# A fused causal attention and PReLU MLP on one core: loads on three queues, a second round of its own, PReLU partly on ScalarE, stores by halves

## The chip, the cores and the metric

One core of one Trainium2 chip. The metric is the device time in microseconds (us) of one execution; each kernel is timed in several runs, and one further execution is profiled. Engines are called PE (TensorE), DVE (VectorE), ACT (ScalarE), POOL (GpSimd) and SP (SyncE, which here only issues DMAs).

## The reference

Causal attention over 4 batches of 12 heads, 448 positions and head size 64, then an MLP on 1792 tokens: 768 inputs, 2048 hidden, PReLU with one slope for each hidden unit, 768 outputs. All in float32.

```python
scores = (1/sqrt(64)) * q @ k.T ; masked above the diagonal with -1e9
attn = exp(scores - max) / (sum + 1e-9)
x = (attn @ v), heads side by side: (1792, 768)
h = x @ w_in
g = maximum(h, 0) + alpha * minimum(h, 0)
out = g @ w_out
```

## The kernel before

**Attention.** The 24 pairs of heads (two heads share the 128 partitions) are worked off in rounds. `ORDER` (L36) is one round's list of steps, each with a lag: `S0+1` in round n is the first scores of pair n - 1, `AV+4` the product with V of pair n - 4. Each engine works in the order in which its instructions are written, so this list is the queue of each engine. `LK` and `LQ` load K and Q on SP (`load`, L345: two DMAs for K, four for Q with its last 64 rows); pair 0's K is issued by ACT. `MXij` is DVE's masked row maximum (L429), `EXij` ACT's exponential with the row sum (L444), `RC` the reciprocal of the sums (L453), `NOij` the normalization on POOL (L398; for the first and the last pair partly on DVE, L460), `PTi` PE's transposes (L472), `Cij` their copies out of PSUM, `AV` the product (L491), `XF`, `XN`, `XH`, `XL` sums, high part and low part of the result. Round 2 uses the same list as the others. `WARM` matmuls on zeros (L338) run before the first scores.

**V.** A batch's V is loaded by seven DMAs (`load_v`, L370), all issued by SP. The first seven follow `LQ` of pair 2; the others are issued in `LV`, by the table `LOADV` (the number after pair p).

**Weights.** Every matmul of the MLP is three matmuls of high and low parts in fp32r. w_in and w_out come as eight-byte numbers, of which pieces of 128x384 are turned to float32 by `start_piece` (L231): an Abs on ACT, a clamp on POOL, four bit operations on DVE (`D`; L249, L253, L256, L257), an add on POOL (`+` or `add`, L260). `cast` (ACT) and `sub` (POOL) make high and low parts. During attention the tables `EARLY`, `FRONT` and `REAR` say in which round this is done (steps `ED`, `E2`, `EA`). `T` makes high and low part of a sum of x (`t_hi`, `t_lo`).

**MLP.** Hidden units come in 8 groups of 256, tokens in two blocks (384 and 512 columns): 16 quads. The first two quads are plain products (`h_plain`), the others seven products per four by sums (`h_step`). `h_act` (L709) makes PReLU of a PSUM bank with two DVE operations (L721, L722), `g_hi` the high part on ACT (L731), `g_lo` the low part on POOL (L735). `o_half` (L758) multiplies with w_out and adds on DVE (L777; for the first group a copy on ACT, L775). `FIRST` is the list of what goes between the products of the first two quads, one row for each product: `act`, `gh`, `gl` ahead of it, the rest behind; `th` and `tl` are the two halves of `T`, on ACT and DVE (L569). With the last group `o_half` stores: a whole row block of 768 columns behind its second half, only the very last block by halves (L778 to L785).

Of the kernel before, what the change touches and what calls it, by code (L numbers as in the profile page):

```python
# [10 lines left out]
F32 = mybir.dt.float32  # L11
# [12 lines left out]
WARM = 9  # L24
EARLY = {
# [92 lines left out]
def kernel(  # L118
# [23 lines left out]
    GC = 2  # L142
# [26 lines left out]
    alpha_sb = const.tile([P, DFF // P], F32, name="alpha_sb")  # L169
    OPS = ["B11", "T1", "T2", "B21", "T3", "B22", "T4"]  # L170
# [410 lines left out]
    plan, front, behind_it = {}, {}, {}  # L581
# [6 lines left out]
    for nm in "qk":  # L588
        steps["L" + nm.upper()] = lambda p, nm=nm: p and load(p, nm)
# [13 lines left out]
    steps["ED"] = lambda p: [fn() for fn in plan.pop(p + 4, ())]  # L603
    steps["LT"] = lambda p: p + 4 < 27 and flush(late)
# [3 lines left out]
    order = []  # L608
    for w in ORDER.split():
        name, lag = w.split("+")  # L610
        if name in choice:
            eng = {"a": nc.scalar, "d": nc.vector, "p": nc.gpsimd}[lag[-1]]
            order.append((int(lag[:-1]), name, lambda p, fn=choice[name], eng=eng: fn(p, eng)))
# [95 lines left out]
    def h_act(q, nm):  # L709
# [11 lines left out]
        ts(out=m, in0=src, scalar1=0.0, scalar2=al, op0=ALU.min, op1=ALU.mult)  # L721
# [36 lines left out]
    def o_half(q, n, t, hf):  # L758
# [105 lines left out]
    def plan_early():  # L864
# [4 lines left out]
        for table, to in ((EARLY, plan), (FRONT, front), (REAR, behind_it)):  # L869
            for n, todo in table.items():  # L870
                for w in todo.split():
# [3 lines left out]
                    if kind == "D":  # L875
                        fns.append(lambda i=int(arg[0]), n=int(arg[1]): ops(name_of(i), 0, n))
# [26 lines left out]
    with tc.manual_schedule():  # L903
# [173 lines left out]
```

## Time and profile before

| | us |
|---|---|
| median of 3 runs | 630.48 (628.66 to 632.01) |
| profiled execution | 627.45 |
| its span | 625.7 |
| PE, DVE, POOL, ACT busy | 608.4, 501.7, 395.7, 277.2 |

The page's first part gives the busy time of each engine; a share near 100% of PE says that PE always had a matmul in work, not that each ran at its fastest. The chain that ended last is 82% PE.

### The profile page before, as it was taken

To read this page: it belongs to the slowest core of one execution; us is meant where nothing else is said; L and a number is where in the kernel's file an instruction comes from. 1 tells how busy PE (TensorE), PEld (TensorE's weight loads), DVE (VectorE), ACT (ScalarE), POOL (GpSimd) and SP (SyncE) were. 2 spreads that over 40 slices of the span, in tenths; PEclk is the share of its full clock that TensorE was granted. 3 is DMA by queue.
4 is the path that set the end of the run, shared out by engine and by line. 5 is a ranking of instruction groups with operands and counts; after the bars stand their busy time and mean duration, and the time that the engine had idled before them with its cause. 6 is when DMAs were issued, how large, how long until landed. Compare 5 with 4: busy or idle time off the path is not lost.

```text
span 625.7 us, 10851 instructions
## 1 busy us (share of the span) xinstructions
PE 608.4 (97%) x3528; PEld 529.6 (85%) x3528; DVE 501.7 (80%) x1117; ACT 277.2 (44%) x766; POOL 395.7 (63%) x530
## 2 busy tenths in 40 slices
PE   7899999999999899999999999999999999999996
PEld 3566676666878799899999999989999999999896
DVE  5699999999688579798689879868977987895363
ACT  5789897898344655231333323232332323232110
POOL 4455676868776758865775687567667766763120
PEclk9899999999999999999999999999999999999999
DMA  5874477642868468656765775786667567554535
GB/s 130 194 184 135 117 223 208 204 134 70 281 188 287 136 207 288 212 181 204 246 190 176 230 215 155 222 250 177 191 221 221 179 218 224 166 175 140 178 137 201
DMA packets 87736, 120.39 MB, mean 192 GB/s; under 512 B 12032, under 2 KB 64256, under 8 KB 87680
## 3 DMA queue, kind: packets, MB, share of 16 engines
q1 hardware_dynamic: 87520, 119.48, 62.6%
q8 instruction: 28, 0.46, 0.3%
q10 hardware_dynamic: 160, 0.23, 0.1%
q14 instruction: 28, 0.23, 0.1%
HBM read 105.00 MB, written 14.68 MB: 191 GB/s over the span
## 4 chain that ended last, share of the span: by engine, by line
PE 82%; DVE 6%; DMA 4%; SPq 3%; POOL 2%; ACT 1%; issue 1%; POOLq 0%; ACTq 0%; DVEq 0%
PE o L769 35%; PE heldY L676 11%; PE heldX L676 8%; PE heldZ L676 5%; PE pt L472 5%; PE a L491 4%; PE s L417 3%; PE h_V L676 3%; PE heldW L676 2%; DMA v<-in_v_dram 2%; PE s L409 2%; SPq L352 2%; ACT p L444 1%; SPq L355 1%; DVE s L429 1%
## 5 line engine op out<-in xcount | busy, mean ns | idle before, releaser
L777 DVE TENSOR_TENSOR acc<-o,acc 128x384 f32<-128x384 f32 x196 | 107.5, 552 | 71.2 <-PE o L769 70.9
L398 POOL TENSOR_SCALAR p<-p,rs 128x128 f32<-128x128 f32 (+3 forms) x164 | 80.4, 512 | 57.2 <-DVE rs L453 34.4
L444 ACT ACTIVATE p<-s,nm 128x256 f32<-128x256 f32 (+3 forms) x168 | 82.0, 497 | 20.1 <-DVE nm L429 19.8
L769 PE MATMUL o<-wo,g_X 128*128 128x384 f32 x336 | 76.8, 335 | 2.9 <-ACT g_X L731 1.8
L769 PE MATMUL o<-wo,g_Z 128*128 128x384 f32 x336 | 76.6, 335 | 1.1 <-DVE t_W L722 0.6
L429 DVE CUSTOM_DVE_ANT_0 s<-s,mask 128x256 f32<-128x256 f32 (+3 forms) x168 | 70.9, 480 | 8.0 <-PE s L417 5.7
L769 PE MATMUL o<-wo,g_W 128*128 128x384 f32 x336 | 76.6, 334 | 0.3 <-POOL g_W L735 0.3
L769 PE MATMUL o<-wo,g_Y 128*128 128x384 f32 x336 | 76.4, 335 | 0.0
L769 PEld LDWEIGHTS o<-wo,g_X 128*128 128x128 f32 x336 | 60.3, 188 | 6.7 <-ACT g_X L731 2.1
L769 PEld LDWEIGHTS o<-wo,g_Z 128*128 128x128 f32 x336 | 60.2, 188 | 4.9 <-DVE t_W L722 0.9
L769 PEld LDWEIGHTS o<-wo,g_W 128*128 128x128 f32 x336 | 59.9, 188 | 0.6 <-POOL g_W L735 0.6
L769 PEld LDWEIGHTS o<-wo,g_Y 128*128 128x128 f32 x336 | 60.0, 188 | 0.0
L491 PEld LDWEIGHTS a<-ptf,v 128*64 128x64 f32 x384 | 27.7, 136 | 35.1 <-issue 10.5
L472 PEld LDWEIGHTS pt<-ident,p 128*128 128x128 f32 x384 | 44.6, 144 | 13.7 <-issue 10.9
L491 PE MATMUL a<-ptf,v 128*64 128x64 f32 (+3 forms) x384 | 49.5, 387 | 3.6 <-DMA v<-in_v_dram 2.3
L472 PE MATMUL pt<-ident,p 128*128 128x128 f32 x384 | 48.7, 279 | 2.4 <-DVE p L460 1.3
L260 POOL TENSOR_TENSOR y_i<-y_i,x_i 128x384 f32<-128x384 f32 x32 | 33.5, 1048 | 27.1 <-DVE x_i L257 27.1
L260 POOL TENSOR_TENSOR y_o<-y_o,x_o 128x384 f32<-128x384 f32 x32 | 32.4, 1012 | 15.9 <-DVE x_o L257 15.9
L394 ACT ACTIVATE ptf<-pt 128x512 f32<-128x512 f32 (+1 forms) x72 | 38.3, 574 | 8.6 <-PE pt L472 8.6
L735 POOL TENSOR_TENSOR g_Z<-t_Z,g_Z 128x384 fp32r<-128x384 f32 (+1 forms) x16 | 20.0, 1247 | 31.1 <-ACT g_Z L731 31.1
L417 PE MATMUL s<-kr,qr 64*128 64x128 f32 (+2 forms) x288 | 38.4, 394 | 0.0
L243 ACT ACTIVATE x_i<-raw_i 128x384 f32<-128x384 f32 x32 | 17.8, 555 | 46.3 <-DMA raw_i<-in_moe_w_in_dram 46.3
(177 smaller groups left out, 1339.4 us busy)
## 6 DMA issues: line engine op xcount, KB each, us to landing
lo_T<-low_T SPq DMA_DIRECT2D x28, 512.0 KB, 4.6
lo_B<-low_B SPq DMA_DIRECT2D x25, 512.0 KB, 4.7
raw_i<-in_moe_w_in_dram SPq DMA_DIRECT2D x32, 384.0 KB, 3.8
raw_o<-in_moe_w_out_dram SPq DMA_DIRECT2D x32, 384.0 KB, 3.3
lo_T<-low_T SPq DMA_DIRECT2D x28, 384.0 KB, 3.9
lo_B<-low_B SPq DMA_DIRECT2D x25, 384.0 KB, 3.9
lo_N<-low_N SPq DMA_DIRECT2D x16, 512.0 KB, 4.8
lo_N<-low_N SPq DMA_DIRECT2D x16, 384.0 KB, 4.5
```

What stands on the lines that cost most here:

```text
L260: nc.gpsimd.tensor_tensor(out=y, in0=y, in1=xf, op=ALU.add)
L394: eng.activation(out, x, AF.Copy, scale=side)
L398: eng.tensor_scalar(out=out, in0=x, scalar1=side, scalar2=1.0, op0=ALU.mult, op1=ALU.mult)
L417: nc.tensor.matmul(ps[:, o : o + lim], T["q", p][half(j), i * QP : (i + 1) * QP], T["k", p][half(j), :lim], start=(o == 0), stop=(n > 0 or ...
L429: nc.vector.tensor_tensor_reduce(out=t, in0=t, in1=masks[1] if i == NQ else masks[0][:, (NQ - 1 - i) * QP :], scale=-SCALE, scalar=MOST_F3 ...
L444: nc.scalar.activation(T["p", p, i][:, j, : t.shape[1]], t, AF.Exp, scale=-1.0, bias=T.pop(("nm", p, i, j)), accum_out=T["sm", p][:, z : z ...
L472: nc.tensor.transpose(ps[:, j - js[0], c], t[:, j, c * QP : (c + 1) * QP], T["ident"])
L491: nc.tensor.matmul(out[half(j), c * QP :], vs[b % 2][:, hp, c, j], x[:, c * QP : S], start=(c == 0), stop=(c == NQ),)
L676: nc.tensor.matmul(ps, w[:, u, k * P : (k + 1) * P], x, start=(first and i == 0), stop=(i == len(mms) - 1), skip_group_check=True,)
L735: nc.gpsimd.tensor_tensor(out=l, in0=hts.pop((q, nm)), in1=h, op=ALU.subtract)
L769: nc.tensor.matmul(ps[:, :NH], x, w, start=(i == 0), stop=(i == 3 * GC - 1))
L777: nc.vector.tensor_tensor(out=a[:, cols], in0=ps[:, :NH], in1=a[:, cols], op=ALU.add)
```

## The change

`WARM` goes from 9 to 8. The K of pair 1 is issued by ACT too. The first four V loads are issued by POOL after `LQ` of pair 1, the other three by SP after `LQ` of pair 2. Round 2 has a list of its own. A new step `EG` takes the first bit operation of a round where the round's work begins with one; `ED` moves behind `RC`. Some entries of `EARLY` and `FIRST` move, and V's last batch is loaded in three rounds. For six of the eight PReLUs of the first group, ACT makes alpha * min(h, 0) as Relu(-h) times -alpha (`less`). `g_lo` of the second quad goes to DVE but for Y. Every half row block is stored as soon as it is done.

```diff
-WARM = 9
+WARM = 8
 EARLY = {
-    13: "+:0 D:1:2 A:2 cast:A21", 14: "C:2 D:1:1 LD D:2:1 +:1", 15: "D:2:2 A:3 T",
-    16: "C:3 sub:A21 D:2:1 LD D:3:1 cast:A22", 17: "D:3:1 T", 18: "+:2 D:3:1 sub:A22 cast:L1", 19: "D:3:1 LD T",
+    13: "+:0 D:1:2 A:2 cast:A21", 14: "D:1:1 C:2 LD D:2:1", 15: "D:2:2 +:1 A:3 T",
+    16: "D:2:1 C:3 sub:A21 LD D:3:1 cast:A22", 17: "D:3:1 T", 18: "D:3:1 +:2 sub:A22 cast:L1", 19: "D:3:1 LD T",
-LOADV = {0: 2, 1: 2, 2: 2, 3: 1, 9: 4, 10: 3, 12: 1, 13: 2, 14: 2, 15: 2}
+LOADV = {0: 2, 1: 2, 2: 2, 3: 1, 9: 4, 10: 3, 12: 2, 13: 3, 14: 2}
 ORDER = """
-... C10+3a MX30+2 XL+4 EX30+2 ED+4 C00+3d C21+3d RC+2 NO01+2p ...
+... C10+3a MX30+2 EG+4 XL+4 EX30+2 C00+3d C21+3d RC+2 ED+4 NO01+2p ...
+SECOND_ROUND = """
+LK+0 LQ+0 MX11+2 EX10+2 EX11+2 MX20+2 MX21+2 EX20+2 MX00+2 EX00+2 EX21+2 MX01+2 EX01+2 MX30+2 S0+1 S1+1 SF+1 MX10+1 MX11+1 EX30+2 RC+2 NO01+2p
+"""
 FIRST = """
 0: gh.0Y gh.0X gl.0Y gl.0X abs.i0.1 clamp.i0.1 cast.o0.0 cast.o1.0
-1: act.0Z gh.0W gl.0W D.i0.1.2 sub.o0.0 sub.o1.0 cast.o2.0 cast.o3.0
-2: gh.0Z gl.0Z D.i0.1.2 load abs.i1.1 clamp.i1.1 sub.o2.0 th
-3: D.i1.1.2 add.i0.1 sub.o3.0 tl th
+1: act.0Z gh.0W gl.0W D.i0.1.2 sub.o0.0 sub.o1.0 cast.o2.0 cast.o3.0 th
+2: gh.0Z gl.0Z D.i0.1.2 load abs.i1.1 clamp.i1.1 sub.o2.0 tl
+3: D.i1.1.2 add.i0.1 sub.o3.0 th
 4: D.i1.1.2 load tl
 5: act.1Y act.1X add.i1.1 th
 6: gh.1Y tl abs.i2.1
-7: gl.1Y clamp.i2.1 S.S1.1 th
-8: D.i2.1.2 tl cast.S1.1
-9: D.i2.1.2 load sub.S1.1 abs.i3.1 cast.L1.1
-10: add.i2.1 clamp.i3.1 sub.L1.1 th
-11: act.1W act.1Z tl
-12: D.i3.1.2 S.S2.1 cast.A22.1
-13: D.i3.1.2 load sub.A22.1 th
-14: add.i3.1 S.S3.1 cast.A11.1 tl
-15: cast.S2.1 sub.A11.1 th
-16: cast.S3.1 sub.S2.1 S.S4.1 tl
-17: gh.1X gl.1X sub.S3.1 abs.o0.1 st
-18: gh.1W gl.1W cast.A12.1 clamp.o0.1
-19: D.o0.1.1 sub.A12.1
-20: D.o0.1.1
-21: D.o0.1.2 load
-22: add.o0.1
+7: gl.1Y clamp.i2.1 S.S1.1
+8: D.i2.1.2 cast.S1.1 th
+9: D.i2.1.2 load sub.S1.1 cast.L1.1
+10: add.i2.1 sub.L1.1 tl abs.i3.1
+11: act.1W act.1Z clamp.i3.1
+12: S.S2.1 cast.A22.1 th
+13: D.i3.1.2 sub.A22.1
+14: D.i3.1.2 load S.S3.1 cast.A11.1
+15: tl cast.S2.1
+16: gh.1X gl.1X add.i3.1 sub.A11.1
+17: gh.1W gl.1W cast.S3.1 sub.S2.1 S.S4.1 th
+18: sub.S3.1 abs.o0.1 cast.A12.1
+19: tl clamp.o0.1 sub.A12.1
+20: D.o0.1.2 th
+21: D.o0.1.2
+22: tl add.o0.1 st load
...
 def load_first():
     load(0, "q")
-    load(0, "k", nc.scalar)
+    for p in range(2):
+        load(p, "k", nc.scalar)
 def load_v(b):
-                nc.sync.dma_start(
+                (nc.gpsimd if b == 0 and n < 2 else nc.sync).dma_start(
 def attention(hooks):
+            for lag, name, fn in second if n == 2 else order:
+                if (n, name) == (3, "MX11"):
+                    continue
 def h_act(q, nm):
-        ts(out=m, in0=src, scalar1=0.0, scalar2=al, op0=ALU.min, op1=ALU.mult)
+        if g == 0 and (bp == 0 or nm in "XY"):
+            nc.scalar.activation(m, src, AF.Relu, scale=-1.0)
+            nc.scalar.activation(m, m, AF.Copy, scale=less[:, OUTS[nm][0] :][:, :1])
+        else:
+            ts(out=m, in0=src, scalar1=0.0, scalar2=al, op0=ALU.min, op1=ALU.mult)
 def g_lo(q, nm):
-        nc.gpsimd.tensor_tensor(out=l, in0=hts.pop((q, nm)), in1=h, op=ALU.subtract)
+        eng = nc.vector if q == 1 and nm != "Y" else nc.gpsimd
+        eng.tensor_tensor(out=l, in0=hts.pop((q, nm)), in1=h, op=ALU.subtract)
 def o_half(q, n, t, hf):
-            if (bp, n, t) == (NBP - 1, 1, blocks[bp][1] // P - 1):
-                wide = [cols]
-            else:
-                wide = [slice(0, DM)] if hf == 1 else []
-            for cs in wide:
-                for part, rows in out_rows(bp, n, t):
-                    nc.sync.dma_start(out=out[rows, cs], in_=a[part, cs])
+            for part, rows in out_rows(bp, n, t):
+                nc.sync.dma_start(out=out[rows, cols], in_=a[part, cols])
 def plan_early():
+                        i, d = map(int, arg)
+                        if to is plan and n < 25 and not fns:
+                            gap[n] = [lambda i=i: ops(name_of(i), 0, 1)]
+                            d -= 1
+                        fns.append(lambda i=i, n=d: ops(name_of(i), 0, n))
-        after(2, "LQ", load_v_some, 7)
+        after(1, "LQ", load_v_some, 4)
+        after(2, "LQ", load_v_some, 3)
+        after(20, "LV", lambda: ts(out=less, in0=alpha_sb[:, :GC], scalar1=-1.0, scalar2=None, op0=ALU.mult))
```

## Rows read from the trace of the kernel before

**Rows 1.** The page's first part: busy us, share of the span, instructions
```profile
PE 608.4 (97%) x3528; PEld 529.6 (85%) x3528; DVE 501.7 (80%) x1117; ACT 277.2 (44%) x766; POOL 395.7 (63%) x530
```
**Rows 2.** Busy us by stage: stretch, length, engines, granted clock, DMA share, GB/s
```profile
78.00:112.00 34.00, 33.49 (x236) 23.59 (x235) 32.05 (x116) 28.64 (x98) 25.26 (x48) 1.00 0.76 217
...
193.00:220.00 27.00, 22.97 (x126) 21.52 (x125) 20.12 (x33) 16.74 (x40) 17.89 (x20) 1.00 0.59 188
```
**Rows 3.** The chain that ended last, 14 to 36 us: start, us, what
```profile
14.44 6.45 DMA v<-in_v_dram
...
21.27 1.20 PE s L409 x2
22.47 3.17 PE pt L472 x16
...
27.14 1.88 PE a L491 x16
...
29.97 1.75 PE pt L472 x16
...
35.10 0.95 PE s L409 x2
```
**Rows 4.** PE in order of time, 0 to 22 us
```profile
1.61 3.66 PE L338 MATMUL warm<-acc 128*128 128x512 bf16 x9 [1.61 <-DVE acc L916]
...
17.34 1.51 PE L491 MATMUL a<-ptf,v 128*64 128x448 f32 x8 [0.66 <-ACT ptf L394]
```
**Rows 5.** ACT in order of time, 3 to 22 us: the second pair's first exponential
```profile
11.37 0.47 ACT L444 ACTIVATE p<-s,nm 128x256 f32<-128x256 f32 x1 [0.92 <-DVE nm L429]
```
**Rows 6.** SP's queue and POOL in order of time, 0 to 30 us
```profile
11.21 3.89 SPq L376 DMA_DIRECT2D v<-in_v_dram  x7
...
11.15 2.54 POOL L398 TENSOR_SCALAR p<-p,rs 128x128 f32<-128x128 f32 x5 [6.51 <-DVE rs L453]
```
**Rows 7.** Busy us by stretches of 4 us at the start
```profile
2.00:6.00 4.00, 4.00 (x19) 1.81 (x19) 0.00 (x0) 1.96 (x4) 2.33 (x8) 1.00 0.59 160
...
14.00:18.00 4.00, 3.24 (x23) 1.74 (x23) 3.00 (x15) 3.95 (x14) 0.98 (x3) 1.00 1.14 216
...
22.00:26.00 4.00, 4.00 (x21) 3.55 (x21) 2.43 (x7) 2.44 (x6) 0.00 (x0) 0.59 0.33 91
```
**Rows 8.** The chain that ended last, 76 to 126 us
```profile
78.32 0.95 PE s L409 x2
...
111.27 0.95 PE s L409 x2
...
119.43 4.61 DMA v<-in_v_dram
...
124.42 0.95 PE s L409 x2
```
**Rows 9.** PE in order of time, 199 to 212 us: its two longest waits
```profile
209.53 0.61 PE L769 MATMUL o<-wo,g_X 128*128 128x384 f32 x2 [1.79 <-ACT g_X L731]
...
211.24 0.45 PE L769 MATMUL o<-wo,g_X 128*128 128x384 f32 x1 [1.11 <-POOL g_X L735]
```
**Rows 10.** DVE and ACT in order of time, 204 to 211 us
```profile
206.89 1.24 DVE L265 TENSOR_TENSOR y_i<-y_i,y_i 128x256 f32<-128x256 f32 x1
...
208.85 0.62 ACT L731 ACTIVATE g_X<-t_X 128x512 fp32r<-128x512 f32 x1
```
**Rows 11.** Two lines' instructions: ns min/median/max, first and last start, forms
```profile
L721 DVE TENSOR_SCALAR t_X<-h_X,alpha_sb x2: 610/677/744, 174.0 to 194.7; 128x384 f32<-128x384 f32 x1, 128x512 f32<-128x512 f32 x1
...
L569 DVE TENSOR_TENSOR acc<-acc,xw x7: 612/896/1220, 191.4 to 208.0; 128x448 fp32r<-128x448 f32 x7
```
**Rows 12.** The end: DVE in order of time, busy us by stretch, landing of L785's stores
```profile
620.36 0.56 DVE L777 TENSOR_TENSOR acc<-o,acc 128x384 f32<-128x384 f32 x1 [0.49 <-PE o L769]
...
621.00:623.00 2.00, 0.00 (x0) 0.00 (x0) 0.00 (x0) 0.00 (x0) 0.00 (x0) 0.90 1.00 371
...
DMA to landing us min/median/max: 1.9/3.0/4.4
```

More of the change, by code (lines that the diff above doesn't have):

```diff
@@ L33 @@
 REAR = {26: "D:7:4 LD +:7"}
-LOADV = {0: 2, 1: 2, 2: 2, 3: 1, 9: 4, 10: 3, 12: 1, 13: 2, 14: 2, 15: 2}
+LOADV = {0: 2, 1: 2, 2: 2, 3: 1, 9: 4, 10: 3, 12: 2, 13: 3, 14: 2}
 TURNS = [(0, 0), (0, 1), (0, 2), (0, 5), (1, 0), (1, 1), (1, 3), (1, 4), (0, 3), (0, 4), (1, 2), (1, 5)]
 ORDER = """
-E2+4 LK+0 LQ+0 LT+4 NO00+3p NO10+3p MX11+2 NO21+3p NO11+3p EX10+2 EX11+2 MX20+2 NO20+3p MX21+2 EX20+2 NO30+3p MX00+2 EX00+2 AV+4 S2+2 LV+4 PT1+3 PT0+3 PT2+3 EX21+2 MX01+2 EX01+2 XF+4 XN+4 XH+4 C10+3a MX30+2 XL+4 EX30+2 ED+4 C00+3d C21+3d RC+2 NO01+2p C20+3a PT3+3 S0+1 S1+1 SF+1 C30+3a EA+4 MX10+1 ST+4
+E2+4 LK+0 LQ+0 LT+4 NO00+3p NO10+3p MX11+2 NO21+3p NO11+3p EX10+2 EX11+2 MX20+2 NO20+3p MX21+2 EX20+2 NO30+3p MX00+2 EX00+2 AV+4 S2+2 LV+4 PT1+3 PT0+3 PT2+3 EX21+2 MX01+2 EX01+2 XF+4 XN+4 XH+4 C10+3a MX30+2 EG+4 XL+4 EX30+2 C00+3d C21+3d RC+2 ED+4 NO01+2p C20+3a PT3+3 S0+1 S1+1 SF+1 C30+3a EA+4 MX10+1 ST+4
+"""
+SECOND_ROUND = """
+LK+0 LQ+0 MX11+2 EX10+2 EX11+2 MX20+2 MX21+2 EX20+2 MX00+2 EX00+2 EX21+2 MX01+2 EX01+2 MX30+2 S0+1 S1+1 SF+1 MX10+1 MX11+1 EX30+2 RC+2 NO01+2p
 """
@@ L169 @@
     alpha_sb = const.tile([P, DFF // P], F32, name="alpha_sb")
+    less = const.tile([P, GC], F32, name="less")
     OPS = ["B11", "T1", "T2", "B21", "T3", "B22", "T4"]
@@ L449, in row_rec @@
     def row_rec(p):
-        sm = T["sm", p]
-        r = T["r", p] = ap["b2"].tile([P, 2 * NQ + 1], F32, tag="rs", name=f"rs_{p}")
+        sm, r = T["sm", p], ap["b2"].tile([P, 2 * NQ + 1], F32, tag="rs", name=f"rs_{p}")
+        T["r", p] = r
         nc.vector.tensor_tensor(out=sm, in0=sm, in1=least, op=ALU.add)
-        nc.vector.reciprocal(r, T.pop(("sm", p)))
+        nc.vector.reciprocal(r, sm)
     def row_norm(p, i, j, eng):
@@ L580 @@
     }
-    plan, front, behind_it = {}, {}, {}
+    plan, front, behind_it, gap = {}, {}, {}, {}
     choice = {}
@@ L588 @@
     for nm in "qk":
-        steps["L" + nm.upper()] = lambda p, nm=nm: p and load(p, nm)
+        steps["L" + nm.upper()] = lambda p, nm=nm: p > (nm == "k") and load(p, nm)
     for n in range(NQ):
@@ L603 @@
     steps["ED"] = lambda p: [fn() for fn in plan.pop(p + 4, ())]
+    steps["EG"] = lambda p: [fn() for fn in gap.pop(p + 4, ())]
     steps["LT"] = lambda p: p + 4 < 27 and flush(late)
@@ L606, with order_of @@
     steps["E2"] = lambda p: [fn() for fn in front.pop(p + 4, ())]
[L608 to L613, printed above, removed]
-        else:
-            order.append((int(lag), name, steps[name]))
-    def attention(hooks):
-        for n in range(len(pairs) + max(lag for lag, *_ in order)):
-            for lag, name, fn in order:
+    def order_of(text):
+        order = []
+        for w in text.split():
+            name, lag = w.split("+")
+            if name in choice:
+                eng = {"a": nc.scalar, "d": nc.vector, "p": nc.gpsimd}[lag[-1]]
+                order.append((int(lag[:-1]), name, lambda p, fn=choice[name], eng=eng: fn(p, eng)))
+            else:
+                order.append((int(lag), name, steps[name]))
+        return order
+    def attention(hooks):
+        order, second = order_of(ORDER), order_of(SECOND_ROUND)
+        last = max(lag for lag, *_ in order)
+        for n in range(len(pairs) + last):
+            for lag, name, fn in second if n == 2 else order:
+                if (n, name) == (3, "MX11"):
+                    continue
                 if 0 <= n - lag < len(pairs):
@@ L720, in h_act @@
             src = t
-        ts(out=m, in0=src, scalar1=0.0, scalar2=al, op0=ALU.min, op1=ALU.mult)
+        if g == 0 and (bp == 0 or nm in "XY"):
+            nc.scalar.activation(m, src, AF.Relu, scale=-1.0)
+            nc.scalar.activation(m, m, AF.Copy, scale=less[:, OUTS[nm][0] :][:, :1])
+        else:
+            ts(out=m, in0=src, scalar1=0.0, scalar2=al, op0=ALU.min, op1=ALU.mult)
         stt(out=t, in0=src, scalar=0.0, in1=m, op0=ALU.max, op1=ALU.add)
@@ L778, in o_half @@
         if g == NG - 1:
-            if (bp, n, t) == (NBP - 1, 1, blocks[bp][1] // P - 1):
-                wide = [cols]
-            else:
-                wide = [slice(0, DM)] if hf == 1 else []
-            for cs in wide:
-                for part, rows in out_rows(bp, n, t):
-                    nc.sync.dma_start(out=out[rows, cs], in_=a[part, cs])
+            for part, rows in out_rows(bp, n, t):
+                nc.sync.dma_start(out=out[rows, cols], in_=a[part, cols])
     in_order = [(c, z) for c in (1, 0) for z in range(2)]
@@ L875, in plan_early @@
                     if kind == "D":
-                        fns.append(lambda i=int(arg[0]), n=int(arg[1]): ops(name_of(i), 0, n))
+                        i, d = map(int, arg)
[3 more added lines that the diff above has]
+                        fns.append(lambda i=i, n=d: ops(name_of(i), 0, n))
                     elif kind == "LD":
```

## The prediction

> **What bounds the kernel now.** I read first the page's busy shares: TensorE (PE) is busy 97% of the span [rows 1], so little beyond its 17 us of idle time, and stretches where it is paced by another engine while counted busy, can be won. Next the busy time by stage: in 193 to 220 us PE has 22.97 of 27 us, so 4.03 are idle there, and in 78 to 112 us DVE has 32.05 of 34 [rows 2]. Then the chain of waits. At the start it goes through the seven loads of V for the first batch: the last lands at 20.89 (14.44 + 6.45), the A·V matmuls of the first pair end at 21.27, and then 16 transposes take 3.17 us where the next round's take 1.75, and the last-row scores 1.20 where later ones take 0.95 [rows 3]: the granted clock is 0.59 of full on average from 22 to 26 us [rows 7], so part of it is at 1.2 GHz. A round of one pair then takes 6.08 us, from 29.02 (27.14 + 1.88) to 35.10 [rows 3], which is PE's own work. From 78.32 to 111.27 five rounds take 32.95, 6.59 each, and the next two, up to 124.42, take 13.15 with a load of V of 4.61 us in the chain [rows 8]. After 220 us PE has no gap worth naming; at the end the stores remain: the last DVE add ends at 620.92, yet the DMA engines are 100% busy from 621 to 623, and the span is 625.7 [rows 12].
>
> The profiled execution took 627.45 us (span 625.7 and 1.75 around it); the median of the three runs is 630.48, so 3.03 above. I subtract the terms from 627.45 and add these 3.03.
>
> **The change part by part.**
>
> 1. *Start.* (a) One warm matmul less: nine take 3.66 us from 1.61 on [rows 4], so 0.41 each; but the first scores need loads that land at about the same moment, so I take 0.3 (ends 0 and 0.41). (b) Issues: on SP's queue stand six issues of K and Q a pair; an issue of V costs 3.89 / 7 = 0.56 there [rows 6], and I price the others by it. The second K (two issues, 1.1) goes to ACT and four of the seven V issues to POOL. Behind the two new issues on ACT wait its table load and the masks; their first user, DVE's masked maximum, waits for PE's scores in any case, so this costs nothing; without that cover up to 1.1. SP then issues the second pair's Q 1.1 earlier, and its three V loads start near 10.1 instead of 11.21 and are out by 11.8. POOL's four can start at 11.15 - 6.51 = 4.64, when its memsets are done: it idles from there to its first normalization [rows 6], which hides the four issues as long as they hold POOL some 6.1 us in all, the normalizations being 0.3 to 0.4 sooner. No row shows POOL issuing a DMA. The low end is SP's price, 2.2 us for four; the high end is that POOL is held as long as one V load is on its way in the chain, 6.45 each. I take 4 us, near SP's, the nearest row for the same load: hidden. (c) Bytes: three pairs of K and Q and V's first batch are about 1344 KB each. By 6 us some 640 KB have moved (160 GB/s over 4 us), and with V in flight the DMA engines reach 216 GB/s at full use [rows 7]; the remaining 2050 KB need 10 us, so V is in at about 16. (d) The order of the second round: MX10 and MX11 of the second pair run on DVE while it waits for the first pair's last exponential, so ACT loses its wait of 0.92 for one of them [rows 5]; since other maxima stay behind the normalizations on DVE, I take 0.85. So the first A·V starts at 17.34 [rows 4] - 0.3 - 0.85 = 16.2 and, with V just landing (I allow 0.35), ends near 18.45 instead of 21.27: 2.8 won. (e) Without the pause before it the clock need not fall: (3.17 - 1.75) + (1.20 - 0.95) = 1.67 more [rows 3]. What is late next is the second pair's normalizations on POOL, seven at 2.54 / 5 = 0.51 [rows 6]: V's delay hid them so far; they move up with the exponentials and end when the scores ahead of their transposes do, at about 19.4 (18.45 + 0.95). Term: 4.5 (ends: 0 and 4.9; with POOL held for long, a loss, below).
>
> 2. *Rounds 12 to 18.* The five slow rounds lose 32.95 - 5 x 6.08 = 2.55 us [rows 8]. The copies C00 and C21 and the reciprocal now stand ahead of the bit operations (step ED), of which the first moves to EG, ahead of the low part; PE waits for the former, for the latter nobody does within the round. But DVE's work is the same, and at 32.05 of 34 us it can give at most 1.95 [rows 2]; its next maxima are now behind the bit operations, which could cost as much as is won. Term 0.7 (ends -1.0 and 1.9).
>
> 3. *V of the last batch.* Its loads are spread over three rounds instead of four, so none is left to the round before its first use. The loss there is 13.15 - 2 x 6.08 = 0.99 [rows 8]; each of the rounds gets one V issue more (0.56), in a queue with some 6 x 0.56 = 3.4 us of other issues in a 6.08 us round. Term 0.9 (ends 0 and 0.99).
>
> 4. *193 to 220 us.* The two long waits of PE, 1.79 and 1.11, are for g_X of the second quad, high part from ACT, then low part from POOL [rows 9]. ACT makes the high part at 208.85, in its queue right behind a cast that waited for DVE's difference of 206.89 to 208.13 [rows 10]; DVE is the late one. Edits: the high and low part of X now stand one row earlier and ahead of that cast; the two L721 operations of the second quad's X and Y, 0.74 each at 128x512 [rows 11], leave DVE for ACT, which idled before them; the residues of the sums (th, tl) are spread, so two fewer of L569's stand on DVE before that point, 0.61 to 1.22 each; against it the low part on DVE, the same operation at 512 columns instead of 448, 0.7 to 1.4 [rows 11]. DVE reaches X's low part near 207, where PE, without its two shorter waits, wants it at about 206.9. The six pairs of ACT operations cost ACT some 7 us in all, of which two pairs fall where it is idle 10.26 of 27 us [rows 2] and the others in the quieter time before; without that cover the copies behind them, which free PE's banks, would be that much later. The chain to g gets one operation longer, where g is used many us later. A table that ACT had to load for Relu would be hidden by the same idle time. Nothing of DVE's remaining list is due before 219. Term 3.0 (ends 0.9 and 4.0).
>
> 5. *End.* Each half row block is stored as it is done, so half of the bytes of the last phase leave during the phase before, and the last store finds the engines free. A store lands 1.9 us after its issue at the least, 3.0 at the median [rows 12]; the last one, issued at about 621, would land near 623.1 and the span end about 1.4 us sooner. The 15 more issues on SP fall where few loads follow that could wait behind them. Term 1.4 (ends 0 and 1.9).
>
> Nothing else in the main loop changes. Sum: 4.5 + 0.7 + 0.9 + 3.0 + 1.4 = 10.5. Then 627.45 - 10.5 + 3.03 = 620.0.
>
> **The rivals.**
> *A. DVE stays the bound.* Term 2 gives nothing, term 4 only the short waits (0.9), and the clock falls all the same since PE still waits for norms and copies between 10 and 16 us: 620.0 + 0.7 + 2.1 + 1.7 = 624.5. For it: DVE has hardly a free microsecond where it matters [rows 2]. Against it: work does leave it, ahead of the wait that costs most.
> *B. POOL pays more for an issue.* At 3 us each, 12 in all, its normalizations start at 16.65, end 2.54 later [rows 6], and with the last transposes and copies (an estimate of 2.0; a round's transposes are 1.75 [rows 3]) and A·V (1.9, as 1.88 in [rows 3]) the first pair ends at 23.1, 1.8 later than now, the clock falling too: 620.0 + 4.5 + 1.8 = 626.3.
> *C. The same, and slower.* If the four issues hold POOL for 22 us (5.5 each, still under the 6.45 end), the first pair ends at 4.64 + 22 + 2.54 + 2.0 + 1.9 = 33.1, 11.8 later, and the whole is 620.0 + 4.5 + 11.8 = 636.3. It outweighs the other four terms (6.0) from 16.2 us for the four on. For it: nothing in the profile shows POOL issuing; the loads are of 512-byte pieces, over 1500 in all. Against: 5.5 us is ten times what SP pays for the same load.
> The Trainium skill, in "SBUF — State Buffer", section "SBUF: two separate sides", speaks for B and C: it says that loads issued from GpSimd have their descriptors written by that engine's own cores, and that VectorE can shut it out while certain copies run, so that a load seems to hang behind VectorE. No row here shows it; by that rule the time would go towards 626 or beyond, though what DVE does in this stretch is mostly the masked maximum and hardly a copy.
> *D. No effect.* V lands no sooner because K and Q of the next pairs share the engines with it, and what is won at 200 us is lost at the next dependence: 628 to 632.
>
> **How the numbers follow.** Forecast 0.50 (own range 616.5 to 623.5: the ends of terms 1 and 4), A 0.25, B 0.12, C 0.07, D 0.06. Up to 628 this holds all but D, C and the far side of B; below 616.5 all terms would have to reach their upper ends. Half a percent (3.15 us) is about what a measurement can tell here: faster is below 627.3, which is the forecast, A and two thirds of B, 0.83; within it D and the rest of B, 0.11; slower 0.06.
>
> **What would show it.** Term 1: A·V of the first pair ends near 18.5, no V load in the chain before 40 us, granted clock 1.00 throughout; POOL's first normalization near 10.8 (later by several us: B or C). Term 2: rounds of pairs 10 to 16 below 6.59. Term 3: no V load in the chain near 120. Term 4: PE busy above 26 of the 27 us behind 189. Term 5: DMA idle between 618 and the end but for single stores, and the last add within 3.5 us of the span's end. The prediction is wrong if POOL is busy for over 10 us with its four loads, or if PE's idle time near 200 us moves instead of going.

## The result, and the profile after

The changed kernel takes 624.08 us (median of six executions, 622.77 to 625.20); the kernel before, on the same chip, 630.43 (six, 628.66 to 632.01). The ratio is 0.9908 [0.9886, 0.9929]: 6.35 us faster, where 10.5 were forecast. That is 4.1 above the forecast of 620.0 and 0.6 above the range that I gave the forecast itself (616.5 to 623.5), but inside the wider one, which runs to 628. The profiled execution took 625.20 us, 2.25 less than that of before; the two lie on opposite sides of their medians (1.1 above, 3.0 below), so the sizes below are read place by place and not from the totals. The places are those of these two executions; of the 6.35 us between the medians they account for 2.25.

The page's first part, as [rows 1]: PE does the same work in a span 2.3 us shorter.

```profile
PE 609.2 (98%) x3527; PEld 532.7 (85%) x3527; DVE 498.9 (80%) x1115; ACT 282.7 (45%) x778; POOL 397.8 (64%) x531
```

Busy time by stretch, as [rows 2] and [rows 7] (the columns are theirs: engines, granted clock, DMA share, GB/s):

```profile
22.00:26.00 4.00, 4.00 (x31) 2.21 (x28) 3.49 (x14) 3.04 (x13) 3.35 (x7) 1.00 0.69 198
74.00:107.00 33.00, 33.00 (x247) 21.93 (x244) 31.73 (x118) 29.32 (x101) 26.37 (x48) 1.00 0.77 222
159.00:168.00 9.00, 9.00 (x59) 8.79 (x58) 2.37 (x5) 2.96 (x6) 4.77 (x7) 1.00 0.84 269
187.00:214.00 27.00, 22.82 (x117) 22.40 (x116) 25.20 (x39) 16.29 (x38) 17.27 (x19) 0.87 0.67 215
198.00:204.00 6.00, 5.84 (x20) 5.87 (x21) 5.86 (x11) 4.56 (x12) 3.78 (x6) 0.55 0.63 181
621.00:623.00 2.00, 0.00 (x0) 0.00 (x0) 0.00 (x0) 0.00 (x0) 0.00 (x0) 1.00 0.27 101
```

Two rows are as forecast: the clock no longer falls at 22 to 26 us, and the DMA engines are mostly free in the last 2 us. The fourth is not: behind 187 us PE is busy 22.82 of 27, no more than before, and the clock falls to 0.55 from 198 to 204, so most of that stretch is at 1.2 GHz. The third is a gap of DVE before it, 2.37 of 9 us busy.

POOL, and PE in order of time at the start, as [rows 4] and [rows 6]:

```profile
4.58 2.79 POOL L381 DMA_DIRECT2D v<-in_v_dram  x4
11.22 2.54 POOL L403 TENSOR_SCALAR p<-p,rs 128x128 f32<-128x128 f32 x5 [3.85 <-DVE rs L458]
```
```profile
10.72 0.99 PE L414 MATMUL s<-kr,qd 128*128 128x448 f32 x2 [1.27 <-DMA qd<-in_q_dram]
...
16.52 1.95 PE L496 MATMUL a<-ptf,v 128*64 128x448 f32 x16 [0.50 <-ACT ptf L399]
```

POOL's four issues take 0.70 us each and are long over when it gets its first normalization. A·V of the first pair ends at 18.47 (it waits for ACT, not for V). But PE now waits 1.27 us for the tail of the second pair's Q, which SP issues at 5.49, behind POOL's first V load at 4.58.

The chain of waits at the start and near 40 us (start, us, what), as [rows 3]:

```profile
18.47 0.95 PE s L414 x2
19.42 1.75 PE pt L477 x16
...
36.61 0.38 SPq L512
...
40.81 3.47 DMA v<-in_v_dram
44.32 0.34 PE a L496 x4
```

The transposes take 1.75 us now, not 3.17 (whether that is the change's doing, e2_before_32 tells). At 40.81 the last load of V's *second* batch is issued, behind a store and six loads of K and Q, and the A·V of the seventh pair waits for it.

PE and DVE in order of time near 160 to 200 us, as [rows 9] and [rows 10]:

```profile
198.16 1.30 PE L786 MATMUL o<-wo,g_Z 128*128 128x384 f32 x3 [4.18 <-DVE t_W L738]
...
203.78 0.68 PE L786 MATMUL o<-wo,g_Z 128*128 128x384 f32 x3
...
206.90 0.68 PE L786 MATMUL o<-wo,g_X 128*128 128x384 f32 x3
```
```profile
165.70 0.42 DVE L401 COPY ptf<-pt 128x256 f32<-128x256 f32 x1 [5.83 <-PE pt L477]
...
168.71 0.35 DVE L253 TENSOR_SCALAR x_o<-x_o 128x384 int32<-128x384 int32 x1
...
179.16 0.56 DVE L738 SCALAR_TENSOR_TENSOR t_Z<-h_Z,t_Z 128x384 f32<-128x384 f32 x1 [3.25 <-ACT t_Z L735]
```

The four waits of before (4.03 us together) have become one of 4.18, for DVE's W and Z of the second quad; then three matmuls take 1.30 us instead of 0.68, at the lower clock. The waits are as long as before in all; what is lost is the clock: the 18 matmuls from 198.16 take 5.62 us, the next 18 3.12, so 2.5 us. DVE is late there although it had idled 5.83 us before 165.70, with four bit operations of a weight piece (first row at 168.71) queued right behind.

The end, as [rows 12] (DVE in order of time; landing of the stores):

```profile
619.79 0.56 DVE L794 TENSOR_TENSOR acc<-o,acc 128x384 f32<-128x384 f32 x1 [0.49 <-PE o L786]
```
```profile
DMA to landing us min/median/max: 1.8/2.1/4.4
```

To see where time was won and lost I take the lead over the kernel before: the start of the same instruction there, minus its start here (us, profiled executions; "pair n" is the start of its last-row scores, pairs counted from 0, "add" an output add of DVE). The last three columns are the span's lead, the stretch from the first add to the last, and the median.

```
               pair 3  pair 6  pair 10  pair 17  pair 23  first add  last add   span  stretch   median
before                                                                                 375.9    630.4
after            4.47    2.96     2.93     5.08     6.07       3.85      0.57   2.25   379.2    624.08
e1_less_128      3.32    2.22     2.20     4.31     5.30       3.79      3.00   4.65   376.7    624.08
e2_before_32     1.94    1.23     1.23     1.34     1.84      -0.14     -3.16  -2.90   378.9    632.38
e3_v_by_sp       2.30    1.18     1.14     2.61     3.57       1.39     -2.08  -0.09   379.4    627.05
e5_fill          3.86    3.39     3.36     5.47     6.47       9.50      6.67   8.35   378.7    619.15
f1_v1_early      3.86    4.22     4.19     6.30     7.29      10.36      7.56   9.23   378.7    618.69
f2_prelu_dve     4.47    4.06     4.03     5.52     6.48       8.45      4.78   6.46   379.6    620.76
f3_wide          3.80    1.78     1.74     3.22     4.19       6.93      3.90   3.70   378.9    621.07
f4_order_before  4.55    2.45     0.74     0.85     1.84       5.39      2.25   3.72   379.0    622.71
g1_best          4.61    4.97     4.93     6.42     7.38      10.07      9.55  11.09   376.4    616.60
g2_less_64       3.87    4.23     4.20     6.34     7.33      11.04      9.53  11.17   377.4    616.84
g3_v1_by_pool    2.70    3.06     3.03     4.53     5.50       7.71      4.27   5.98   379.3    618.58
```

Read along the row of after: +4.47 at the start, -1.5 at pair 6, +2.15 from pair 10 to 17, +1.0 at pair 18, -2.2 from attention's end to the first add, then 3.3 lost bit by bit in the main loop, and +1.7 in the stores. Eight runs have the start of after unchanged up to here (after, e1, e5, f1, f2, f3, f4, g2); their leads at pair 3 run from 3.32 to 4.55, so a difference of 1 us between two runs there says nothing.

### The profile page after: what moved, and what is told of

Its sections match the earlier page's. It is cut to its first block, busy times and chain, and to the rows that moved or that the text cites. A ratio compares the mean times of both kernels' runs of the same rounds, so it can differ in the third digit from the quotient of the medians.

```text
span 623.4 us, 10906 instructions
## 1 busy us (share of the span) xinstructions
PE 609.2 (98%) x3527; PEld 532.7 (85%) x3527; DVE 498.9 (80%) x1115; ACT 282.7 (45%) x778; POOL 397.8 (64%) x531
## 4 chain that ended last, share of the span: by engine, by line
PE 89%; DVE 4%; DMA 2%; POOL 1%; ACT 1%; issue 1%; SPq 1%; POOLq 0%; DVEq 0%; ACTq 0%
PE o L786 37%; PE heldY L688 11%; PE heldX L688 8%; PE a L496 6%; PE pt L477 6%; PE heldZ L688 5%; PE s L422 5%; PE s L414 3%; PE heldW L688 3%; PE h_V L688 3%; DVE s L434 1%; ACT p L449 1%; DMA low_N<-low_N 1%; DMA lo_N<-low_N 1%; PE warm L342 1%
## 5 line engine op out<-in xcount | busy, mean ns | idle before, releaser
L786 PE MATMUL o<-wo,g_Z 128*128 128x384 f32 x336 | 79.1, 344 | 4.2 <-DVE t_W L738 4.2
L786 PE MATMUL o<-wo,g_W 128*128 128x384 f32 x336 | 78.4, 340 | 0.3 <-POOL g_W L752 0.3
L786 PEld LDWEIGHTS o<-wo,g_Z 128*128 128x128 f32 x336 | 61.8, 191 | 7.6 <-ACT wi_A L291 4.5
L786 PEld LDWEIGHTS o<-wo,g_W 128*128 128x128 f32 x336 | 61.7, 191 | 0.6 <-POOL g_W L752 0.6
L496 PEld LDWEIGHTS a<-ptf,v 128*64 128x64 f32 x384 | 25.3, 136 | 33.3 <-issue 11.8
L477 PEld LDWEIGHTS pt<-ident,p 128*128 128x128 f32 x384 | 43.1, 141 | 11.8 <-issue 7.9
L496 PE MATMUL a<-ptf,v 128*64 128x448 f32 (+3 forms) x384 | 47.0, 386 | 2.2 <-DMA v<-in_v_dram 1.7
L477 PE MATMUL pt<-ident,p 128*128 128x128 f32 x384 | 47.0, 274 | 1.1 <-POOL p L403 0.7
L264 POOL TENSOR_TENSOR y_o<-y_o,x_o 128x384 f32<-128x384 f32 x32 | 32.8, 1024 | 22.4 <-DVE x_o L261 20.6
L422 PE MATMUL s<-kr,qr 64*128 64x256 f32 (+2 forms) x288 | 38.6, 395 | 0.0
L752 POOL TENSOR_TENSOR g_Z<-t_Z,g_Z 128x384 fp32r<-128x384 f32 (+1 forms) x15 | 18.5, 1232 | 31.4 <-ACT g_Z L747 31.4
```

What stands on the lines that cost most here:

```text
L264: nc.gpsimd.tensor_tensor(out=y, in0=y, in1=xf, op=ALU.add)
L422: nc.tensor.matmul(ps[:, o : o + lim], T["q", p][half(j), i * QP : (i + 1) * QP], T["k", p][half(j), :lim], start=(o == 0), stop=(n > 0 or ...
L477: nc.tensor.transpose(ps[:, j - js[0], c], t[:, j, c * QP : (c + 1) * QP], T["ident"])
L496: nc.tensor.matmul(out[half(j), c * QP :], vs[b % 2][:, hp, c, j], x[:, c * QP : S], start=(c == 0), stop=(c == NQ),)
L786: nc.tensor.matmul(ps[:, :NH], x, w, start=(i == 0), stop=(i == 3 * GC - 1))
```

## The experiments

Four questions were open: whether POOL's issuing is what helped at the start; why DVE is late near 196 us; why the seventh pair waits for V; and why the main loop, whose instructions are the same, is 3.3 us longer. On the last, the output matmuls of one block start every 173.8 ns before and every 177.5 after (mean of some 700 each, 250 to 600 us). The new tile `less`, 32 bytes a partition, stands ahead of the big tiles in the program and so, by the order of their allocation, moves all of them by 32 bytes. The runs come from three chips, on which the kernel before took 630.59 us (the e runs), 630.12 (f) and 630.04 (g); each ratio is to it on the same chip, and medians of different letters compare to some 0.5 us only.

**e1_less_128**: the changed kernel, `less` 128 bytes wide.

```diff
-    less = const.tile([P, GC], F32, name="less")
+    less = const.tile([P, 32], F32, name="less")[:, :GC]
```


> The changed kernel with its new tile `less` 128 bytes wide a partition instead of 32, so that every later tile of SBUF stands 128 bytes behind its place in the kernel before instead of 32. Theory P (placement): the 32 bytes make the 128x384 matmuls start every 176.7 ns instead of 173.7; the stretch from the first add of the main loop's output on DVE to the last (375.9 us before, 379.2 in the changed kernel) comes back to about 376, and the median falls by 3.3, to 620.8 (ratio to before 0.985). Rival R: the pace differs from execution to execution whatever the placement; the median stays within 1 us of 624.1 and the stretch is anything from 375 to 380.

The output matmuls start every 173.7 ns again and the stretch is 376.7. The median, 624.08 (ratio to before 0.9891 [0.9867, 0.9915]), did not move: this start lost 1.15 us against after (PE waited 2.28 us for the second pair's Q, the clock was 0.96 in the first 40 us), and over the timed executions the gain is not resolved.

**e2_before_32**: the kernel before with an unused tile in the place of `less`.

```diff
     alpha_sb = const.tile([P, DFF // P], F32, name="alpha_sb")
+    less = const.tile([P, GC], F32, name="less")
```


> The kernel before with an unused tile of 32 bytes a partition in the place of `less`, and nothing else. Theory P (placement): the stretch from the first output add to the last goes from 375.9 to about 379.2 and the median from 630.4 to 633.7 (ratio 1.005). Rival R (pace by execution): ratio 1.000 within 0.001, the stretch anything from 375 to 380.

632.38, ratio 1.0028 [1.0011, 1.0046]; pitch 177.5 ns, stretch 378.9. One unused tile costs 3.0 us in the trace and 1.8 (0.7 to 2.9) in the median. Groups of instructions by line (busy us, mean ns of one), first of the kernel before, then of this one:

```profile
L769 PE MATMUL o<-wo,g_Y 128*128 128x384 f32 x336 | 76.4, 335 | 0.0
```
```profile
L770 PE MATMUL o<-wo,g_Y 128*128 128x384 f32 x336 | 77.9, 340 | 0.0
```

The same 336 matmuls, with no wait in front of them in either, are 5 ns longer each. Theory P holds in the trace both ways and R falls; in the median the tile costs about half of what P said (ratio 1.005).

This run also has the old start, with the same loads of V and nearly the same wait for them (1.4 us, 1.6 in before). The chain, and the stretch that was at 0.59 in [rows 7]:

```profile
14.44 6.18 DMA v<-in_v_dram
...
21.95 1.75 PE pt L473 x16
```
```profile
22.00:26.00 4.00, 4.00 (x34) 2.78 (x34) 3.65 (x14) 3.14 (x9) 1.48 (x4) 1.00 0.35 89
```

The clock does not fall here, and pair 3 starts 1.94 us sooner than in the profiled execution of before, with nothing done to the start. So 1.67 of the lead of 4.47 (4.47 at pair 3 against 2.80 at pair 2) is the clock of that one execution of before and no gain that the change is shown to make; how many of the timed executions of before have it, no trace here shows. Behind 205 us it is the other way round: from 205 to 214 us the clock is 0.81 here and 1.00 in before, and 1.98 us of lead go between pair 23 and the first add.

**e3_v_by_sp**: POOL's share given back to SP.

```diff
-                (nc.gpsimd if b == 0 and n < 2 else nc.sync).dma_start(
+                nc.sync.dma_start(
...
-        after(1, "LQ", load_v_some, 4)
-        after(2, "LQ", load_v_some, 3)
+        after(2, "LQ", load_v_some, 7)
```


> The changed kernel with all seven first loads of V issued by SP behind the third pair's Q, as before; the second K stays on ACT and the second round's order stays. Theory E (the early issue on a free engine is what counts): SP issues V from about 10.5 to 14.4 us, the last lands near 20, A.V of the first pair ends near 20.4 instead of 18.47, the granted clock falls once more, the lead over the kernel before at pair 3's last-row scores is 0.5 to 1.5 us instead of 4.47, and the median is 627 to 628. Rival O (bytes and the second round's order count, not who issues): the lead stays at 3.5 or more and the median within 1 us of 624.1.

627.05, ratio 0.9949 [0.9928, 0.9969], 3.0 above the changed kernel. PE in order of time:

```profile
19.55 0.55 PE L496 MATMUL a<-ptf,v 128*64 128x192 f32 x4 [1.34 <-DMA v<-in_v_dram]
20.30 0.34 PE L496 MATMUL a<-ptf,v 128*64 128x64 f32 x4 [0.20 <-DMA v<-in_v_dram]
```

A·V of the first pair stands with its matmuls waiting for V again and ends near 20.6; the lead at pair 3 is 2.30. So of the 4.47, 2.2 is POOL's issuing (1.0 to 2.3 against the eight runs with its start; 3.0 in the median). Of the other 2.3, 1.67 is the clock that fell in before and not here (the transposes behind took 1.91 in this view, as in later rounds), and about 0.6 is left for the second K on ACT, the second round's order and the warm matmul, which no run separates. Theory E holds for the end of A·V and the median; that the clock would fall again was wrong, and with it the lead of 0.5 to 1.5.

The run settles one thing more. SP issues the tail of the second pair's Q at 5.42 and 5.93 us, as in the changed kernel (5.49 and 6.00). Here, with no V from POOL ahead of it, it lands at 7.37 and 7.91 instead of 10.31 and 10.59, and PE does not wait for it:

```profile
9.33 1.02 PE L414 MATMUL s<-kr,qd 128*128 128x448 f32 x2
```

**e5_fill**: one clamp and the four bit operations of round 26 ahead of the copies.

```diff
-    ... 26: "C:6 C:7 D:6:4 LD T T +:6 T T",
+    ... 26: "C:7 LD T T +:6 T T",
+GAP = {26: "C:6 D:6:4"}
...
-        for table, to in ((EARLY, plan), (FRONT, front), (REAR, behind_it)):
+        for table, to in ((EARLY, plan), (FRONT, front), (REAR, behind_it), (GAP, gap)):
```


> The changed kernel with one clamp and four bit operations (C:6 and D:6:4 of round 26) put ahead of the copies C00 and C21 again, where DVE idles 5.83 us (159.9 to 165.7). Theory F (these operations, moved behind copies that wait for PE, make DVE late at 196 us): DVE reaches the second quad's W and Z 2.5 to 4 us sooner, PE's wait of 4.18 us near 198 falls below 1.5, the clock does not fall there, and the median is 620.5 to 621.5. Rival G (ACT's Relu and Copy, for which DVE waits 3.25 us at 179, are the cause): the wait stays above 3 and the median within 1 us of 624.1.

619.15, ratio 0.9827 [0.9800, 0.9855]: 4.9 below the changed kernel, and 1.4 below the expected 620.5. DVE, then PE, in order of time, and the stretch behind 187 us:

```profile
159.66 0.36 DVE L254 TENSOR_SCALAR x_o<-x_o 128x384 int32<-128x384 int32 x1 [0.85 <-POOL x_o L251]
...
175.39 0.56 DVE L739 SCALAR_TENSOR_TENSOR t_Z<-h_Z,t_Z 128x384 f32<-128x384 f32 x1 [0.32 <-ACT t_Z L736]
```
```profile
194.43 0.77 PE L787 MATMUL o<-wo,g_Z 128*128 128x384 f32 x3 [0.87 <-DVE t_W L739]
```
```profile
187.00:214.00 27.00, 26.13 (x149) 25.43 (x148) 22.97 (x35) 19.20 (x47) 17.63 (x20) 1.00 0.64 198
```

The four operations fill the gap; DVE's wait of 3.25 us for ACT goes with it, since POOL, which ACT waited for, gets its piece earlier too (its add behind these operations starts at 164.66 instead of 170.72). PE waits 0.87 instead of 4.18 and the clock stays at its upper level. The lead over this stretch goes from -2.2 to +3.03 (9.50 - 6.47). Theory F holds; G falls.

**f4_order_before**: the changed kernel with ED ahead of the copies in all rounds and EG empty.

```diff
-... MX30+2 EG+4 XL+4 EX30+2 C00+3d C21+3d RC+2 ED+4 NO01+2p ...
+... MX30+2 XL+4 EX30+2 ED+4 C00+3d C21+3d RC+2 NO01+2p ...
...
-                        if to is plan and n < 25 and not fns:
+                        if False:
```


> The changed kernel with the bit operations (ED) ahead of the copies C00 and C21 in every round again, as before, and nothing split off into EG. Theory F (moving ED behind the copies wins time in rounds 12 to 18 and loses it after attention): the rounds of pairs 11 to 16 go back to 6.4 to 6.9 us, so 2 us of lead are lost there; PE's wait near 198 falls below 1.5; the median is 621 to 622.5. Rival T (the rounds became faster by the order of the table EARLY and not by ED's place): they stay near 6.08 and the median is 619 to 620. Rival G (ACT's PReLU makes the wait): it stays above 3 and the median is 625 to 627.

622.71, ratio 0.9889 [0.9848, 0.9930], 0.2 above Theory F's range. From pair 10 to 17 the lead rises by 0.11 (0.74 to 0.85) instead of 2.15, five of the seven rounds being 6.38 to 6.83 us again; from attention's end to the first add it rises by 3.55. PE's waits up to 215 us (releaser: total, times, longest):

```profile
PE a L496 <- DMA v<-in_v_dram: 2.2, 1, 2.2
...
PE o L786 <- DVE t_W L738: 0.9, 1, 0.9
```

So the place of the bit operations (ED, with its part EG) won term 2 and lost term 4. T and G fall.

The next three start from the kernel of e5_fill, the last three from that of f1_v1_early.

**f1_v1_early**: V's second batch issued one round earlier.

```diff
-LOADV = {0: 2, 1: 2, 2: 2, 3: 1, ...
+LOADV = {0: 2, 1: 3, 2: 2, ...
```


> The kernel of e5_fill with the seven loads of V's second batch issued in three rounds instead of four (3 in the second of them, none in the fourth). Theory V (the last of them, issued near 40.8 us, lands at 44.3 and holds the A.V of pair 6 up): the round of pair 6, 7.56 us in the changed kernel and 6.91 in e5_fill, goes to 6.08, no load of V stands in the chain near 44, and the lead gained (0.5 to 1.5) stays to the end of attention. Rival S (SP's queue is the late one: the loads of K and Q wait behind the added issue): the round of pair 6 or the one before it stays 0.5 or more above 6.08. The median moves by less than 1 either way.

618.69, ratio 0.9825 [0.9794, 0.9857]. All rounds from pair 3 to 13 are 6.08 to 6.10; the lead at pair 6 is 4.22 where e5_fill has 3.39. Theory V holds, Rival S falls. The late load costs what SP's queue makes of it: against before, 1.5 us in after, 0.5 in e5_fill, 2.0 in f3_wide, whose first rounds are the same.

**f2_prelu_dve**: the first operation of PReLU back on DVE.

```diff
-        if g == 0 and (bp == 0 or nm in "XY"):
+        if False:
```


> The kernel of e5_fill with the first operation of PReLU back on DVE for the first group, as before: six pairs of Relu and Copy less on ACT, four operations of 0.61 and two of 0.74 more on DVE (3.9 us) between 165 and 192. Theory H (DVE is the bound there, so giving them to ACT was worth its time): PE's wait for the second quad's W and Z, 0.9 in e5_fill, is 2.5 to 4.5, with the clock falling, and the median 621.5 to 623.5. Rival I (they fit into what DVE idles, 2.3 us near 172 and the 1.1 it waits for ACT): the wait stays under 2 and the median is 619 to 620.5.

620.76, ratio 0.9855 [0.9823, 0.9887]. PE's waits behind attention are 1.5 us in all (0.7, 0.6, 0.2), and the lead rises by 1.97 up to the first add instead of 3.03. The clock does not fall. The wait is as Rival I said, the median between the two ranges: ACT's share of PReLU is worth about 1 us there.

**f3_wide**: whole row blocks stored, as before.

```diff
-            for part, rows in out_rows(bp, n, t):
-                nc.sync.dma_start(out=out[rows, cols], in_=a[part, cols])
+            ...
+                wide = [slice(0, DM)] if hf == 1 else []
```


> The kernel of e5_fill with the output stored a whole row block at a time, as before. Theory W (half of the bytes of the end leave earlier when stored by halves): the span ends 5.3 us behind the last output add's start instead of 3.6, and the median is 620.9. Rival: the stores by halves gain nothing, what differs comes from elsewhere: 3.6 and 619.2.

621.07, ratio 0.9856 [0.9819, 0.9893]. The span ends 5.52 us behind the start of the last add (621.97 - 616.45), in e5_fill 3.63, in before 5.31. Theory W holds: 1.9 us.

**g2_less_64**: f1_v1_early with `less` 64 bytes wide (`[P, 16]`).

> f1_v1_early with `less` 64 bytes wide instead of 32. Theory P64 (what counts is the address within 64 bytes): pitch 173.7 ns, stretch about 376, median 616 to 617.5. Rival P128 (it is the address within 128 bytes): pitch 176.7 or another value, stretch 378 to 380, median 618 to 619.5.

616.84, ratio 0.9794 [0.9762, 0.9825], 1.85 below f1_v1_early and 1.74 below g3_v1_by_pool, which has the 32 bytes (and V's second batch on POOL) and ran on the same chip. The pitch is 174.4 ns and the stretch 377.4: most of it back, not all. The median is P64's; pitch and stretch lie a little above it, so the address within 64 bytes isn't the whole of it.

**g3_v1_by_pool**: V's second batch by POOL too.

```diff
-                (nc.gpsimd if b == 0 and n < 2 else nc.sync).dma_start(
+                (nc.gpsimd if b == 0 and n < 2 or b == 1 else nc.sync).dma_start(
```


> f1_v1_early with the seven loads of V's second batch issued by POOL too, between 20 and 40 us, where DVE is busy 27.57 of 30 us (at the start it idles much of the time). Theory Q (an issue costs POOL what it did at the start, 2.79 / 4 = 0.7 us, whatever DVE does): seven instructions of 0.5 to 1.0 us, the rounds of pairs 3 to 7 stay at 6.08, the median within 1 us of 618.7. Rival K (DVE's work keeps POOL from writing descriptors): 2 us or more each, POOL's normalizations late, these rounds 0.5 to 3 us above 6.08 each, the median 621 or more.

618.58, ratio 0.9831 [0.9789, 0.9872]. POOL in order of time, and the stretch (DVE is the third of the engines):

```profile
20.23 1.32 POOL L382 DMA_DIRECT2D v<-in_v_dram  x2
27.08 2.02 POOL L382 DMA_DIRECT2D v<-in_v_dram  x3
33.36 1.32 POOL L382 DMA_DIRECT2D v<-in_v_dram  x2
```
```profile
20.00:40.00 20.00, 20.00 (x153) 13.52 (x150) 17.43 (x65) 17.45 (x61) 15.38 (x30) 1.00 0.75 222
```

0.67 us each with DVE busy 17.43 of 20, and rounds of 6.08. Theory Q holds, Rival K falls. The lower lead of this run was lost ahead of these issues, at pair 2 (1.03 against 2.19 in f1_v1_early), where the clock was at 0.57 from 14 to 18 us, 1.00 in f1_v1_early.

**g1_best**: f1_v1_early, `less` 128 bytes wide, and the tail of the second pair's Q issued by POOL ahead of V.

```diff
-                eng.dma_start(out=qd[p % 3][half(j), j * LQ : (j + 1) * LQ], in_=src[:, j, w:])
+                (nc.gpsimd if p == 1 else eng).dma_start(out=qd[p % 3][half(j), ...
```


> f1_v1_early with `less` 128 bytes wide and the two loads of the second pair's tail of Q issued by POOL ahead of its four loads of V. Placement: the stretch from the first output add to the last goes from 378.7 to about 376 and the matmuls of the output start every 173.7 ns instead of 176.7. Start: the tail of Q lands near 7 us instead of 10.4, PE doesn't wait for it (1.2 us in f1_v1_early), and the lead at pair 3's last-row scores is 4.3 to 5 instead of 3.86. Median 615 to 616.5, against 618.7. Rival: POOL's two more issues make its first normalization later than 11.3 and the lead at pair 3 falls below 3.9; and the placement shows in the trace alone, the median staying above 617.5.

616.60, ratio 0.9789 [0.9755, 0.9823]. POOL in order of time:

```profile
4.73 1.26 POOL L360 DMA_DIRECT2D qd<-in_q_dram  x2
5.98 2.62 POOL L382 DMA_DIRECT2D v<-in_v_dram  x4
11.10 2.53 POOL L404 TENSOR_SCALAR p<-p,rs 128x128 f32<-128x128 f32 x5 [2.50 <-DVE rs L459]
```

PE no longer waits for Q there; the lead at pair 3 is 4.61, and POOL is still idle for 2.50 us before its first normalization. The median is 0.1 above the expected range and as that of g2_less_64. With all repairs the change is worth 13.4 us instead of 6.4.

## Why the prediction was right or wrong

1. *Start, 4.5: the path of V right, the clock not shown.* The lead is 4.47, but it has two parts. A·V of the first pair ends at 18.47 (18.45 said) instead of 21.27, which is 2.8; that the end came out so exactly is partly luck, since A·V starts at 16.52 and not at 16.2, and the 0.35 allowed for V was not needed. The other 1.67 stands under (e): "Without the pause before it the clock need not fall". In e2_before_32 the clock stays up with that pause and in the old kernel, so this is a difference between executions that I put down as a gain. POOL's four issues take 2.79 us (4 said, SP's price 2.2). Inside the sum, the warm matmul gave nothing (the scores start 0.05 us sooner), and a wait that I had not seen came: 1.27 us for the second pair's Q, which lands behind POOL's V (e3_v_by_sp). Rivals B and C needed 3 to 5.5 us an issue; the longest single one took 0.96. The rule of the Trainium skill that was weighed there ("SBUF — State Buffer", section "SBUF: two separate sides") did not decide: the issues cost no more beside a busy DVE (g3_v1_by_pool). Whether DVE ran the copies in question at that moment, no run here shows. "No V load in the chain before 40 us" was true, and one stands there at 40.81: the second batch's, to whose place in SP's queue I gave no thought. 1.5 us went there.

2. *Rounds 12 to 18, 0.7: the mechanism right, the size too small.* 2.15. I limited it by DVE's free time and subtracted for the maxima that now stand behind the bit operations. DVE is as full as before (31.73 of 33), yet five of the seven rounds from pair 10 on take PE's own 6.08: what counted was the order of its operations. f4_order_before shows that the place of ED and EG did it. The order has a small price, too: in five runs (e3, f2, f3, g1, g3) the bit operation that now stands ahead of the low part near 107 us takes 1.79 us instead of 1.10, PE waits 0.4 for that low part, and one round takes 6.71.

3. *V of the last batch, 0.9: as said.* 1.0 at pair 18, and PE waits for no V load there in any run with the new table. No run tests this term by itself; e2_before_32, with the old table, loses 0.5 there.

4. *193 to 220 us, 3.0: wrong, -2.2.* The step that failed stands in term 2: "PE waits for the former, for the latter nobody does within the round". In round 26 the copies wait nearly 6 us for transposes that PE reaches only at 164.84, behind matmuls of the first group. Before, DVE did four bit operations in that time; now they stand behind the copies, and 28 us later DVE is late for W and Z. PE's waits in this stretch are as long as before (4.18 against 4.03), and the clock behind the one long wait costs 2.5 us more. This is the sign of being wrong that the prediction named: "if PE's idle time near 200 us moves instead of going". I had looked at the move in the rounds where it helps and not in the last. What term 4 itself said was right: with these operations back in their place, by either way, the stretch gives 3.03 (e5_fill) or 3.55 (f4_order_before) against the one execution of before (e2_before_32, the old code, takes 2.0 more there), of which ACT's share of PReLU is about 1 (f2_prelu_dve). What the other moves in `FIRST` and `g_lo` on DVE are worth was not separated.

5. *End, 1.4: right.* 1.7 in the trace, 1.9 by f3_wide.

"Nothing else in the main loop changes" was the other failure. By instructions it is true; the 32 bytes of `less` made it 3.3 us longer in the trace (1.8 in the median by e2_before_32).

The sum of the signed parts is +4.47 - 1.5 + 2.15 + 1.0 - 2.2 - 3.3 + 1.7 = 2.3, that of the profiled executions. It leaves out what the prediction added at the end, 3.03 for the median above the profiled execution: in the changed kernel the median lies 1.1 below it, in e5_fill 0.06 above, so this was no constant to carry over. Nor does the range of the forecast, 616.5 to 623.5, follow from the ends of terms 1 and 4, as was said; these give 618.6 to 626.6. With the repairs (the four bit operations, the width of `less`, V's second batch) the time is 616.6 to 616.8, below the 620.0: so the gains were larger than the 10.5 said, and the losses that I had at nothing hid it. In the traces term 2 gave 1.45 more than said; where the rest of the difference lies is not shown. Of rival A, 624.5, the time was right and the reason was not: term 2 gave more, not nothing, and DVE was late by its order, not by its load.

## What to carry to other kernels

An operation moved behind another on an in-order engine is moved behind what that one waits for, and in the first and last rounds of a pipeline this is something else than in the middle: each round's queue has to be read, not the typical one. And one profiled execution of each kernel is not enough where the clock is a term of the sum: another execution of the old code shows whether it falls there each time. A load moved to an idle queue starts earlier and by that gets ahead of loads that somebody needs sooner. And a new small tile moves all that stand behind it: compare the pitch of unchanged instructions, and pad the tile if it changed.

## What the runs showed of the hardware

- *Placement.* The output matmuls of one block start every 173.7 to 173.8 ns in the three kernels with the large tiles at their old place or 128 bytes behind it, every 177.4 to 177.5 in the nine with 32 bytes, and every 174.4 in the one with 64. Which tile's address counts was not separated, nor why the median shows about 2 us where the trace shows 3.
- *POOL's price for issuing a load*: 0.65 to 0.70 us on the mean, against 0.56 on SP for the same loads.
- *The clock behind a wait.* Behind PE's wait of 4.2 us near 198 us the granted clock falls in all three traces that have it (0.63, 0.72 and 0.54 on average from 199 to 205 us in after, e1_less_128 and e3_v_by_sp); behind e5_fill's of 0.87 it stays at 1.00. Behind the wait for V near 20 us it falls in before (0.59 from 22 to 26 us) and stays at 1.00 in e2_before_32 and e3_v_by_sp. So a wait can cost more than its length, though not in every execution: e5_fill's is 3.3 us shorter than after's, and the lead of that stretch grows by 5.25. Over 23 executions of the kernel before, time went from 628.5 us at a mean granted clock of 0.995 to 633.1 at 0.987; e5_fill had 1.000 in four of five.
